# A fused attention and feed-forward kernel: the middle of its written-out order replaced

## The chip, the cores and the metric

The kernel runs on one core of one Trainium2 chip. The metric is device time in microseconds (us) of one execution. A core has five engines that run side by side, each with its own queue of instructions, executed in order: TensorE (PE, with its weight loads as PEld), VectorE (DVE), ScalarE (ACT), GpSimd (POOL) and SyncE (SP). SP and GpSimd issue nearly all DMA transfers here. An engine that waits for a semaphore holds up everything behind it in its own queue.

## The reference

Eight batches of eight heads, 576 positions, head size 64. Each batch goes through Nystrom attention with 32 landmarks, and all results through a two-layer feed-forward net with a SiLU between.

```python
q_lm = q.reshape(B, H, 32, S // 32, D).mean(axis=3)
k_lm = k.reshape(B, H, 32, S // 32, D).mean(axis=3)
A  = softmax(scale * q    @ k_lm.T)
Bm = softmax(scale * q_lm @ k_lm.T)
C  = softmax(scale * q_lm @ k.T)
Z = Bm.T / (norm1(Bm) * norminf(Bm) + 1e-6)
for _ in range(6):
    Z = 2 * Z - Z @ Bm @ Z
x = (A @ Z @ C @ v)              # -> 4608 tokens x 512
h = x @ w_in                     # 512 x 2048
out = (h * sigmoid(h)) @ w_out   # 2048 x 512
```

## The kernel before

All work is cut into named steps, and the order of all steps is written out by hand in one string, `SEQUENCE`. `Plan.run` reads it word by word. A word is a step's name, a dot and its batch; a slash gives the engine where a step may run on two; `<x` adds a wait for the step x (a gate). Each engine gets its steps in the order in which they stand in the string, and `tc.manual_schedule` emits them so; true data dependences are added by the framework as semaphore waits. The string fixes which of the eight PSUM banks a product gets.

The steps of batch b that matter here, with the lines of their code:

- `ldTGH.b` (L400): GpSimd loads half (H) of head group G of k (T=1) or q (T=0), 144 KB, cast to bf16 on the way, into the buffer `qk` that batches b and b+2 share. `ldvA.b` (L417) loads a third of v, 192 KB.
- `xtTG.b` (L553): SP issues a DMA transpose of one loaded group into `qT`. Batches 0 to 2 transpose on TensorE instead.
- `lraT`, `lrbT`, `lrcT`, `lrdT` (L592): four adds on DVE that sum `qT` to the landmarks of k or q; each `lraT` needs both groups of T. `ltrT` and `sb` on TensorE, `lmT` (a copy) and `pb` (ACT, exp) follow.
- `pbs`, `pbr`, `bmx`, `bmt`, `bbd`, `n1`, `nrm`, `stf`, `stz` (DVE): the normalised Bm and the start of the inverse. Then six rounds of `fbI` (DVE, L702), `nsI` (TensorE) and `nsdI` (DVE, L727).
- `A`, `C` (TensorE), `Ax`, `Cx` (ACT, exp), `S` (TensorE, row sums), `Ln`, `Rs` (ACT) and `etn` (DVE, L778): the two softmaxes.
- `ctG.b` (L831): SP issues a DMA transpose of the exponentials `ce` into `ct`. `cv` (TensorE) multiplies them by v; `wc` (DVE, L862) scales the result; `zbd` (DVE), `zt` (TensorE) and `ztc` (a copy) join it with the inverse; `mF` (TensorE) multiplies by w_in, and `mcFG` copies its two halves to `m`.
- `hN.b` (TensorE, two products of 512 columns) and `hx`: the first layer, `m` times `etn`. `gN`, `gx` (ACT, L932, L955): SiLU.
- `ssI`, `p1` to `p7`, `c1`, `u2`, `c5`, `c11`, `c12`, `c21`, `c22` (L1029 to L1087): the second layer, by Strassen's seven products of eight matmuls with 256 columns for each pair of token tiles. `@5320` names batch 3, pair 20. `os@` (L1000) is a group of four stores of 64 KB each, issued by SP, from one of eight buffers `ost`.

Around the change the order has a habit: the kinds of transfer take turns. `xt` and `ct` are gated on the last load before them, and the first load of a group on a transpose before it (`ld100.5<xt10.4`, `xt11.5<ldv1.5`). Gates are emitted as a dependence whose reason is given in the code as "one kind of transfer at a time":

```python
for x in o.after:
    tc.add_manual_dep(o.ins, x.ins.name, ..., reason="one kind of transfer at a time")
```

Of the kernel before, what the change touches and what calls it, by code (L numbers as in the profile page):

```python
# [65 lines left out]
ld111.4 c11@5120.0 os@5101.0 ldv1.4<xt00.3 ns00.3 m0.2 mc01.2/DVE ld000.4<xt00.3 p7@5120.0 ld001.4
nsd00.3 h4.2 c5@5120.0/DVE fb10.3 c22@5120.0 Rs0.3 Rs1.3 h7.2 wrc.3 ns10.3 ld010.4 g7.2 ld011.4
h10.2 mc00.2/ACT p4@5120.0 c21@5120.0/ACT nsd10.3 fb20.3 ns20.3 nsd20.3 ldv0.3 os@5100.0 h5.2
h14.2 g5.2 fb30.3 ns30.3 hx0.2 h8.2 g10.2 ldv2.3 gx0.2 h15.2 nsd30.3 fb40.3 g8.2 h12.2 g12.2
ldv2.4<xt00.3 g15.2 ct1.3<ldv1.4 ns40.3 nsd40.3 ct0.3<ldv1.4 xt00.4<ldv1.4 h9.2 g9.2 g14.2 h1.2  # L70
h0.2 g1.2 g0.2 fb50.3 ss30@5120.0 ns50.3 nsd50.3 zbd.3 h11.2 g11.2 h13.2 h3.2 cv0.3 h2.2 wc.3 g4.2
g13.2 g3.2 etn1.3 zt.3 ztc.3/DVE etn0.3 p3@5120.0 c12@5120.0 m3.3 mc30.3/ACT m0.3 mc01.3/DVE
mc00.3/ACT m2.3 mc21.3/ACT m1.3 mc20.3/ACT hx8.2 g2.2 h6.2 g6.2 mc31.3/DVE h12.3 gx8.2 h3.3 h10.3
mc10.3/DVE mc11.3/DVE h7.3 h2.3 g2.3 h4.3 g4.3 g10.3 h13.3 h5.3 g5.3 hx8.3 gx8.3 g13.3 h9.3 h11.3
g7.3 h14.3 h6.3 g6.3 g11.3 p1@5200.0 g3.3 h8.3 g8.3 ss00@5200.0 p5@5200.0 hx0.3 g14.3 g9.3
ss00@5220.0 xt11.4<ldv1.4 xt01.4<ldv1.4 xt10.4<ldv1.4 ld100.5<xt10.4 ld101.5 ld110.5 ld111.5
ldv0.4 ldv1.5 ld000.5 ld001.5 ld010.5 ld011.5 ss10@5200.0 lra1.4 lrb1.4 lrc1.4 ss10@5220.0
ss20@5220.0 lrd1.4 lra0.4 lrb0.4 os@5020.0 ss20@5200.0 l1done.2 ltr1.4 h1.3 h0.3 g0.3 g1.3 g12.3
h15.3 gx0.3 c1@5200.0/DVE p6@5200.0 u2@5200.0/ACT os@5021.0 ss30@5200.0 c5@5200.0/DVE p3@5200.0
ss30@5220.0 lmT1.4/DVE lrc0.4 lrd0.4 ltr0.4 lmT0.4/ACT g15.3 p1@5220.0 sb.4 pb.4 c1@5220.0/ACT  # L80
xt11.5<ldv1.5 xt10.5<ldv1.5 c12@5200.0 p7@5200.0 c22@5200.0 p2@5200.0 c11@5200.0 p4@5200.0
c21@5200.0/ACT p6@5220.0 xt01.5<ldv1.5 pbs.4 u2@5220.0/ACT pbr.4 l1done.3 bmx.4 bmt.4 bbd.4
ss00@5300.0 xt00.5<ldv1.5 C.4 lra1.5 csb.4 os@5120.0 Cx10.4 os@5121.0 Cx00.4 f0.4 p5@5220.0 Cx11.4
p7@5220.0 n1.4 lrb1.5 lrc1.5 os@5200.0 Cx01.4 nrm.4 ct0.4<ldv1.5 lrd1.5 c5@5220.0/ACT stf0.4 A.4
Ax00.4 Ax01.4 p5@5300.0 ltr1.5 fb00.4 Ax10.4 p3@5220.0 S10.4 Ln10.4 Ax11.4 wrc.4 stz.4 p1@5300.0
ns00.4 ss10@5300.0 ss20@5300.0 ss30@5300.0 c1@5300.0/ACT S00.4 S11.4 c22@5220.0 lra0.5 p4@5220.0
Ln11.4 Rs1.4 p6@5300.0 nsd00.4 lrb0.5 lrc0.5 lrd0.5 S01.4 fb10.4 lmT1.5/DVE ld000.6<xt00.5 ltr0.5
p2@5220.0 u2@5300.0/ACT p7@5300.0 ss00@5320.0 Ln01.4 c12@5220.0 lmT0.5/DVE sb.5 c21@5220.0/ACT
ns10.4 p1@5320.0 Ln00.4 ld001.6 ld010.6 Rs0.4 ld011.6 ct1.4<ldv1.5 ldv0.5<ct1.4 ldv2.5 ld100.6
ld101.6 ld110.6 ld111.6 etn1.4 pb.5 ss20@5320.0 c11@5220.0 etn0.4 pbs.5 pbr.5 p2@5320.0 nsd10.4  # L90
c1@5320.0/ACT fb20.4 bmx.5 c11@5320.0 c5@5300.0/ACT p3@5300.0 c12@5300.0 c22@5300.0 C.5 Cx01.5
cv0.4 wc.4 ldv1.6<xt00.5 bmt.5 Cx11.5 ns20.4 os@5201.0 p6@5320.0 nsd20.4 fb30.4 os@5221.0
ss10@5320.0 A.5 os@5220.0 ss30@5320.0 Cx10.5 u2@5320.0/ACT p5@5320.0 Ax11.5 csb.5 Ax01.5 bbd.5
ns30.4 Ax10.5 p7@5320.0 nsd30.4 S11.5 fb40.4 ns40.4 Ax00.5 p1@5340.0 n1.5 nrm.5 stz.5 f0.5 nsd40.4
Ln11.5 c5@5320.0/ACT fb50.4 S10.5 Ln10.5 ns50.4 ss00@5340.0 p3@5320.0 p4@5300.0 stf0.5 c22@5320.0
Rs1.5 S00.5 S01.5 Cx00.5 nsd50.4 fb00.5 Ln01.5 c12@5320.0 ns00.5 ss20@5340.0 zbd.4 p2@5300.0 zt.4
nsd00.5 fb10.5 ns10.5 c11@5300.0 p4@5320.0 wrc.5 c21@5300.0/ACT etn1.5 nsd10.5 p5@5340.0 fb20.5
Ln00.5 l1done.7 ct0.5 ztc.4/ACT c1@5340.0/ACT c21@5320.0/ACT Rs0.5 ss10@5340.0 m3.4 mc30.4/ACT
m1.4 mc31.4/DVE m2.4 mc21.4/ACT p6@5340.0 mc11.4/DVE ns20.5 mc20.4/ACT p2@5340.0 nsd20.5
mc10.4/ACT h5.4 fb30.5 ns30.5 c5@5340.0/DVE nsd30.5 h7.4 h4.4 h9.4 ct1.5 u2@5340.0/ACT g5.4 g7.4  # L100
fb40.5 ns40.5 nsd40.5 fb50.5 p7@5340.0 ss30@5340.0 ns50.5 nsd50.5 c22@5340.0 h14.4 h12.4 g4.4
zbd.5 m0.4 g9.4 g12.4 mc00.4/ACT mc01.4/DVE cv0.5 wc.5 h11.4 h1.4 g11.4 g14.4 c11@5340.0
xt00.6<ldv1.6 zt.5 p3@5340.0 ztc.5/DVE etn0.5 g1.4 ldv0.7<xt00.6 c12@5340.0 ldv1.7<xt00.6 m0.5
ldv2.7<xt00.6 ld100.7<xt00.6 ld101.7 mc01.5/ACT m3.5 mc00.5/ACT ld110.7 ld111.7 m1.5 ldv2.6<xt00.5
mc10.5/ACT xt10.6<ldv1.6 l1done.6 xt11.6<ldv1.6 ldv0.6<xt00.5 ld000.7<xt00.6 mc11.5/DVE h0.4 h10.4
mc30.5/DVE h13.4 ld001.7 g10.4 g13.4 h4.5 ld010.7 g0.4 h15.4 h7.5 g15.4 ld011.7 xt01.6<ldv1.6 h6.4
g6.4 mc31.5/DVE h14.5 h2.4 h8.4 g4.5 os@5320.0 g2.4 lra1.6 lrb1.6 os@5301.0 lrc1.6 lrd1.6 lra0.6
lrb0.6 g7.5 ltr1.6 h15.5 lrc0.6 m2.5 lmT1.6/DVE lrd0.6 g8.4 h3.4 h12.5 hx0.4 g3.4 mc21.5/DVE hx0.5
mc20.5/DVE h8.5 ss00@5400.0 gx0.4 ss20@5400.0 ss10@5400.0 gx0.5 h2.5 g2.5 h11.5 hx8.5 ltr0.6 g11.5
g8.5 p4@5340.0 h1.5 h5.5 g15.5 g12.5 gx8.5 lmT0.6/DVE sb.6 g14.5 g5.5 os@5300.0 hx8.4  # L110
c21@5340.0/DVE ss00@5420.0 p1@5400.0 gx8.4 p5@5400.0 ss30@5400.0 c1@5400.0/ACT p6@5400.0 l1done.5
ss20@5420.0 ss30@5420.0 ss10@5420.0 c5@5400.0/DVE pb.6 u2@5400.0/DVE A.6 Ax00.6 Ax11.6 p3@5400.0
h3.5 Ax01.6 pbs.6 pbr.6 bmx.6 csb.6 p1@5420.0 Ax10.6 h13.5 n1.6 g13.5 os@5321.0 c1@5420.0/DVE
h10.5 nrm.6 g10.5 p7@5400.0 h9.5 c12@5400.0 stz.6 bmt.6 bbd.6 S01.6 g3.5 S10.6 c22@5400.0 g1.5
f0.6 stf0.6 fb00.6 h6.5 h0.5 ns00.6 p6@5420.0 g9.5 xt00.7<ldv1.7 nsd00.6 fb10.6 ns10.6 g0.5 g6.5
u2@5420.0/ACT S00.6 nsd10.6 p5@5420.0 fb20.6 Ln10.6 ns20.6 p7@5420.0 c5@5420.0/ACT ss00@5500.0
xt10.7<ldv1.7 ss20@5500.0 S11.6 nsd20.6 Ln01.6 ss10@5500.0 Ln11.6 xt01.7<ldv1.7 xt11.7<ldv1.7
fb30.6 os@5341.0 p4@5400.0 Ln00.6 Rs0.6 c22@5420.0 c21@5400.0/ACT lra1.7 lrb1.7 lrc1.7 lrd1.7
lra0.7 lrb0.7 lrc0.7 os@5340.0 lrd0.7 C.6 Cx00.6 Cx11.6 Cx01.6 Cx10.6 wrc.6 p1@5500.0 Rs1.6
c1@5500.0/ACT p3@5420.0 c12@5420.0 p2@5500.0 p2@5420.0 ltr1.7 ns30.6 lmT1.7/ACT c11@5500.0  # L120
ct1.6<ldv1.7 ltr0.7 p4@5420.0 lmT0.7/ACT sb.7 p6@5500.0 nsd30.6 fb40.6 c11@5420.0 pb.7
c21@5420.0/ACT etn0.6 ss00@5520.0 ns40.6 etn1.6 A.7 pbs.7 u2@5500.0/ACT Ax01.7 Ax10.7 p5@5500.0
p7@5500.0 Ax00.7 S10.7 S01.7 c5@5500.0/ACT S00.7 ct0.6<ldv1.7 nsd40.6 Ln10.7 p2@5400.0 ss30@5500.0
fb50.6 ns50.6 pbr.7 bmx.7 Ln00.7 bmt.7 Ln01.7 csb.7 nsd50.6 n1.7 zbd.6 os@5401.0 Ax11.7 bbd.7
c11@5400.0 cv0.6 wc.6 c22@5500.0 C.7 nrm.7 p3@5500.0 Cx01.7 zt.6 f0.7 Cx11.7 ztc.6/ACT Cx10.7
ss20@5520.0 stf0.7 p4@5500.0 Cx00.7 c12@5500.0 S11.7 Ln11.7 ss10@5520.0 m1.6 os@5400.0 m0.6 m2.6
mc20.6/ACT mc21.6/ACT mc11.6/ACT mc10.6/DVE mc00.6/DVE p1@5520.0 wrc.7 stz.7 fb00.7 p2@5520.0
ns00.7 mc01.6/ACT nsd00.7 p5@5520.0 fb10.7 c1@5520.0/ACT ns10.7 Rs0.7 ct0.7 c11@5520.0 p6@5520.0
c5@5520.0/ACT nsd10.7 fb20.7 ns20.7 c21@5500.0/DVE h0.6 h5.6 h7.6 nsd20.7 h10.6 Rs1.7 g5.6 h3.6
ct1.7 etn1.7 fb30.7 ns30.7 g7.6 ss30@5520.0 os@5501.0 h4.6 nsd30.7 u2@5520.0/ACT g10.6 g0.6 hx0.6  # L130
fb40.7 ns40.7 nsd40.7 fb50.7 p7@5520.0 ns50.7 m3.6 g4.6 c22@5520.0 gx0.6 nsd50.7 cv0.7 wc.7 zbd.7
# [1060 lines left out]
```

## Time and profile before

| | us |
|---|---|
| median of 3 runs | 239.73 |
| lowest, highest | 238.82, 241.90 |
| the profiled execution | 238.85 |
| its span (first to last instruction) | 237.1 |

The profiled execution is 1.75 us longer than its span, for what lies around it. The page of the profile gives busy time by engine, the span in forty slices, the DMA queues, the chain of work that ended last and the costliest groups of instructions. Views of the trace give windows, waits, or instructions in order of time, and for DMA the time from issue to landing. The names in them are the program's tiles: `qT<-qk` is an `xt`, `ct<-ce` a `ct`, `qk<-in_k_dram` a load of k, `v<-in_v_dram` a load of v, `out_dram<-ost` a store, `red<-qT` an `lra`, `fb<-st` an `fb`, `ps<-etn,m` an `h`, `ps<-v,ct` a `cv`.

### The profile page before, as it was taken

The numbers are of one execution on the slowest core, as the hardware profiler recorded it, in microseconds if no ns is written. First come the engines' busy times: TensorE is split into PE (matmuls) and PEld (weight loads), VectorE is DVE, ScalarE is ACT, GpSimd is POOL, SyncE is SP. The second block draws the span as 40 slices with busy tenths as digits, with TensorE's granted clock in tenths as the row PEclk, the third lists the DMA queues.
The fourth block names the chain that finished last, engine by engine and source line by source line (L and its number), as shares of the span: only waits on it lengthen the run. The fifth ranks groups of instructions, "written<-read, shape, count | busy, mean of one in ns | idle before, by whom it ended". The sixth has DMA issues, their size and how long they took to land.

```text
span 237.1 us, 7501 instructions
## 1 busy us (share of the span) xinstructions
PE 230.2 (97%) x2951; PEld 167.6 (71%) x2951; DVE 182.2 (77%) x506; ACT 182.4 (77%) x435; POOL 49.3 (21%) x89
## 2 busy tenths in 40 slices
...
DMA  6999999999999998999999999995427440012355
GB/s 248 268 202 195 203 211 206 207 202 210 130 182 181 215 171 168 204 198 173 211 163 187 182 164 232 206 180 113 100 59 108 117 113 0 4 44 48 82 144 131
DMA packets 56227, 37.72 MB, mean 159 GB/s; under 512 B 36992, under 2 KB 47744, under 8 KB 56192
## 3 DMA queue, kind: packets, MB, share of 16 engines
...
q8 instruction: 23, 0.38, 0.7%
...
## 4 chain that ended last, share of the span: by engine, by line
PE 77%; ACT 8%; DMA 6%; DVE 4%; issue 2%; SPq 1%; DVEq 0%
PE ps L334 75%; DMA out_dram<-ost 4%; ACT gm L932 2%; DMA gm<-in_k_dram 2%; PE ps L526 1%; DVE etn L778 1%; ACT L1145 1%; ACT m L344 1%; ACT L932 1%; ACT pb L658 1%; DVE zt L346 1%; ACT gx L955 0%; DVE st L727 0%; ACT ce L804 0%; SPq L1000 0%
## 5 line engine op out<-in xcount | busy, mean ns | idle before, releaser
L932 ACT ACTIVATE gm<-ps 128x512 f16<-128x512 f32 x128 | 68.4, 630 | 6.7 <-PE ps L334 6.4
L334 PE MATMUL ps<-etn,m 128*128 128x64 bf16 (+2 forms) x566 | 71.5, 275 | 0.3
L334 PEld LDWEIGHTS <-gm 128*128 128x128 f16 x512 | 48.7, 98 | 10.2 <-issue 1.5
L334 PE MATMUL ps<-w_out_sb,gm 128*128 128x256 f16 (+1 forms) x392 | 53.1, 281 | 0.1
L334 PEld LDWEIGHTS <-m 128*128 128x128 bf16 x566 | 36.7, 98 | 22.2 <-issue 2.6
L334 PEld LDWEIGHTS <-ss 128*128 128x128 f16 x408 | 38.4, 98 | 7.2 <-issue 1.9
L334 PE MATMUL ps<-wt,ss 128*128 128x256 f16 x272 | 34.9, 273 | 0.0
L1064 DVE TENSOR_TENSOR ost<-ost,ps 128x256 f32<-128x256 f32 x51 | 20.6, 414 | 11.3 <-PE ps L334 8.0
L344 ACT COPY ost<-ps 128x256 f32<-128x256 f32 (+1 forms) x47 | 18.1, 391 | 11.8 <-PE ps L334 11.5
L346 DVE CAST m<-ps 128x512 bf16<-128x512 f32 x30 | 19.5, 685 | 3.3 <-PE ps L334 3.2
L417 POOL DMA_DIRECT2D v<-in_v_dram x24 | 14.4, 608 | 34.9 <-PE ps L334 16.4
L344 ACT CAST m<-ps 128x512 bf16<-128x512 f32 x34 | 18.5, 607 | 2.4 <-PE ps L334 2.4
L727 DVE SCALAR_TENSOR_TENSOR st<-st,ps 128x128 bf16<-128x128 bf16 (+2 forms) x54 | 13.6, 257 | 7.7 <-PE ps L334 7.3
L334 PE MATMUL ps<-w_out_sb,ss 128*128 128x256 f16 x136 | 17.6, 273 | 0.0
L400 POOL DMA_DIRECT2D qk<-in_k_dram x20 | 10.6, 548 | 29.8 <-DMA qT<-qk 16.7
L334 PE MATMUL ps<-wt,gm 128*128 128x256 f16 x120 | 15.5, 272 | 0.0
L702 DVE TENSOR_TENSOR fb<-st,hmask 128x256 bf16<-128x256 bf16 (+1 forms) x54 | 14.4, 273 | 1.2
L955 ACT ACTIVATE gx<-ps 128x512 f16<-128x512 f32 x16 | 9.9, 623 | 6.9 <-PE ps L334 6.9
L346 DVE COPY ost<-ps 128x256 f32<-128x256 f32 x23 | 9.6, 419 | 7.0 <-PE ps L334 6.6
L400 POOL DMA_DIRECT2D qk<-in_q_dram x20 | 10.6, 556 | 20.4 <-issue 12.0
L804 ACT ACTIVATE ce<-ps 128x288 bf16<-128x288 f32 x32 | 13.0, 434 | 2.3 <-PE ps L334 2.3
L769 ACT ACTIVATE ln<-ps 128x288 f32<-128x288 f32 x32 | 12.4, 448 | 2.8 <-PE ps L334 2.8
...
## 6 DMA issues: line engine op xcount, KB each, us to landing
...
```

Source lines behind the costliest of these rows:

```text
L334: nc.tensor.matmul(out=out_ap, lhsT=lhsT, rhs=rhs, start=start, stop=stop, skip_group_check=True)
L344: return nc.scalar.copy(out=out, in_=in_)
L346: return nc.vector.tensor_copy(out=out, in_=in_)
L400: lambda e, t=t, g=g, h=h, src=src: nc.gpsimd.dma_start(out=qk_r[b % 2][64 * h:64 * h + 64, t, g].rearrange("p j d -> p (j d)"), in_=src[b ...
L417: lambda e, a=a: nc.gpsimd.dma_start(out=v_r[b % 2][a * L:(a + 1) * L, :, :], in_=v[b].rearrange("h (l a x) d -> a l h (x d)", l=L, a=VA)[ ...
L702: nc.vector.tensor_tensor(out=fb[it % 2][:, g0:g1], in0=bc(sr[it % 3][:, g0:g1, 0:L], 4, 2), in1=bc(hmask, n, 1), op=OP.mult), [o], 14.5 + ...
L727: nc.vector.scalar_tensor_tensor(out=s2[:, g0:g1, lo:SW], in0=s[:, g0:g1, lo:SW], scalar=2.0, in1=ps[:, 0:NG * SW].rearrange("p (g x) -> p ...
L769: lambda e, g=g, c=c, ln=ln: nc.scalar.activation(out=ln[:, c], in_=bank(me["S", g, c])[:, 0:HS], func=AF.Ln),
L804: nc.scalar.activation(out=ce[:, :, 0:VP].rearrange("p (i c) (a l) -> p c a i l", c=2, a=VA)[:, c], in_=bank(me["C"], 2 * g + c)[:, 0:HS]. ...
L932: lambda e, dc=dc, cell=cell: nc.scalar.activation(out=gm[:, dc, :], in_=bank(cell["o"]), func=AF.Silu),
L955: lambda e, d0=d0, cell=cell, c=c: nc.scalar.activation(out=gx[:, d0:d0 + 8, c:c + 64].rearrange("p d (x c) -> p d x c", c=2) if b >= B - ...
L1064: nc.vector.tensor_tensor(out=out_, in0=x, in1=y, op=OP.add)
```

## The change

Only the string `SEQUENCE` changes, and in it the words from just behind `C.3 zt.2` to `ldv1.6`, before `h11.4`. By the times of the profile that is from 70 to 136 us. No step is added or left out; the words before and behind are the same.

- Loads and stores: the first ten loads go out in another order, with new gates. `ld111.6` stands behind them and in front of batch 5's loads; it overwrites what `xt11.4` reads. `ld111.5` is gated on `xt01.4`. Loads of batch 6 stand among those of batch 5, and `ldv0.4` is gated on the store `os@5120.0`.
- Transposes: `xt11.4` and `xt10.4` come first, then two store groups, then `xt01.4` and `xt00.4`; `xt00.4` is gated on `ld111.6`. In batch 5 the pairs come as `xt10 xt11`, a store group, `xt01 xt00`. `ct0.3` is gated on `ld111.4`.
- Some gates name transfers that ended long before, such as `ldk10`, a load at the very start.
- Twenty evictions from PSUM change engine: eleven from DVE to ACT, nine from ACT to DVE.
- Products stand in another order: `cv0.3` has nine `h` of batch 2 ahead of it in place of fourteen; `cv0.4` stands behind `ns50.4` in place of `C.5`; the pair products of batches 2 and 3 are spread otherwise.
- On DVE `lra1.4` and `lrb1.4` stand ahead of `etn0.3`, and `lra0.5` to `lrc0.5` ahead of `stf0.4`.

What each of the two DMA queues issues, from the first difference (cut to the changed words):

```diff
 SP
-os@5001.0 os@5000.0 os@5101.0 os@5100.0 ct1.3<ldv1.4 ct0.3<ldv1.4 xt00.4<ldv1.4 xt11.4<ldv1.4
-xt01.4<ldv1.4 xt10.4<ldv1.4 os@5020.0 os@5021.0 xt11.5<ldv1.5 xt10.5<ldv1.5 xt01.5<ldv1.5
-xt00.5<ldv1.5 os@5120.0 os@5121.0 os@5200.0 ct0.4<ldv1.5 ct1.4<ldv1.5 os@5201.0 os@5221.0
-os@5220.0 ct0.5 ct1.5
+os@5001.0 os@5000.0 ct0.3<ld111.4<ld000.4 os@5101.0 ct1.3 xt11.4<ld010.4 xt10.4<ld010.4 os@5100.0
+os@5020.0 xt01.4<ld010.4 xt00.4<ld111.6<ldv2.3 os@5021.0 xt10.5<ld101.6 xt11.5<ld111.6 os@5121.0
+xt01.5 xt00.5<ld001.5 os@5120.0 ct1.4<ld011.6 ct0.4<ld011.6 os@5220.0 os@5221.0 os@5200.0
+ct1.5<ldv2.5<ldv0.5 os@5201.0 ct0.5<ld011.5
 xt00.6<ldv1.6 xt10.6<ldv1.6
 POOL
 ld100.4<ct0.2
-ld101.4 ld110.4 ld111.4 ldv1.4<xt00.3 ld000.4<xt00.3 ld001.4 ld010.4 ld011.4 ldv0.3 ldv2.3
-ldv2.4<xt00.3 ld100.5<xt10.4 ld101.5 ld110.5 ld111.5 ldv0.4 ldv1.5 ld000.5 ld001.5 ld010.5 ld011.5
-ld000.6<xt00.5 ld001.6 ld010.6 ld011.6 ldv0.5<ct1.4 ldv2.5 ld100.6 ld101.6 ld110.6 ld111.6
-ldv1.6<xt00.5
+ld000.4<ldk10 ld001.4<xt01.3<ldk10 ld101.4<ldk11<xt00.3 ld111.4<os@5001.0 ld011.4<xt00.3
+ld110.4<os@5000.0<xt00.3 ldv0.3<os@5000.0<ldk00 ld010.4<os@5001.0 ldv2.3<ldk00<xt10.3
+ld111.6<os@5101.0 ld000.5 ld111.5<xt01.4<os@5101.0 ld110.5<os@5001.0 ld101.6<xt10.4
+ld001.5<xt10.4<ct0.3 ldv1.4<xt00.4<os@5000.0 ld101.5<ct1.3 ld100.5<os@5101.0
+ld011.5<os@5101.0<os@5021.0 ld010.5<os@5000.0 ld011.6<xt11.4<os@5101.0 ldv2.4<os@5021.0
+ldv0.4<os@5120.0 ld000.6 ldv2.5 ld110.6<xt11.5<xt00.5 ldv0.5<os@5121.0 ld100.6<os@5121.0<xt00.5
+ldv1.5<xt00.5 ld010.6<xt11.5<xt01.5 ld001.6<ct0.4 ldv1.6
 ldv0.7<xt00.6
```

And DVE's order at the two places that the prediction follows:

```diff
-wc.3 etn1.3 ztc.3 etn0.3 c12@5120.0 mc01.3 mc31.3 mc10.3 mc11.3
+wc.3 c12@5120.0 lra1.4 lrb1.4 etn0.3 mc31.3 mc30.3 lrc1.4 lrd1.4 lra0.4
...
-lra1.5 n1.4 lrb1.5 lrc1.5 nrm.4 lrd1.5 stf0.4 fb00.4
+lra1.5 lrb1.5 n1.4 nrm.4 lrc1.5 bmt.4 c22@5220.0 bbd.4 lrd1.5 ss00@5320.0 lra0.5 lrb0.5 lrc0.5
+stf0.4 fb00.4
```

180 lines of the change are left out of this document (92 added, 88 removed).

## The prediction

> **What bounds the kernel now.** The page first: span, engines, DMA. Then the windows table over most of the stretch that the change rewrites (70 to 140 us).
>
> ```profile
> span 237.1 us, 7501 instructions
> PE 230.2 (97%) x2951; PEld 167.6 (71%) x2951; DVE 182.2 (77%) x506; ACT 182.4 (77%) x435; POOL 49.3 (21%) x89
> DMA  6999999999999998999999999995427440012355
> ```
>
> ```profile
> 85.00:90.00 5.00, 4.66 (x108) 2.47 (x107) 3.48 (x7) 4.38 (x10) 0.00 (x0) 1.00 1.20 186
> 90.00:140.00 50.00, 50.00 (x632) 36.60 (x629) 42.98 (x119) 40.50 (x102) 14.30 (x27) 1.00 1.06 183
> ```
>
> TensorE is the bound: busy 97% of the span at the full granted clock. The columns of the second view are window, its length, then busy time of PE, PEld, DVE, ACT and POOL, the clock, the DMA share and GB/s. DMA is full too: its share is above 1 in both windows, so transfers queue behind each other. An order that leaves the products as they are can only win what TensorE still waits. The waits of the weight loads show that better than busy PE, because a matmul's modelled end hides a short stall (70 to 140 us):
>
> ```profile
> PEld L334 <- DVE wsb L862: 0.9, 2, 0.7
> PEld L334 <- DVE fb L702: 0.5, 2, 0.3
> PEld L334 <- DMA ct<-ce: 0.5, 1, 0.5
> PEld L334 <- ACT m L344: 0.3, 1, 0.3
> PEld L334 <- DVE pbs L667: 0.2, 1, 0.2
> PEld L334 <- DVE zt L346: 0.2, 1, 0.2
> ```
>
> Together 2.6 us, 1.1% of the span. That is the most the change can give. By the busy PE row it would be 0.34 us (5.00 less 4.66). The Trainium skill (Trainium Kernel Development and Optimization, Performance Expectations) calls matmul busy time a bad metric for the distance to the roofline; the two sums here agree with that. What TensorE waits for longest stands in the timeline:
>
> ```profile
> 82.80 1.46 PE L334 MATMUL ps<-etn,m 128*128 128x512 bf16 x6
> 85.68 0.44 PEld L334 LDWEIGHTS <-ct 96*32 96x32 bf16 x48 [0.53 <-DMA ct<-ce]
> 87.00 0.11 PEld L334 LDWEIGHTS <-wsb 128*128 128x128 bf16 x2 [0.72 <-DVE wsb L862]
> ```
>
> The value product cv.3 waits 0.53 us for the transposed ct.3; zt.3, right after it, waits 0.72 us for the eviction of cv.3 (wc.3).
>
> **What is moved, queue by queue.** No instruction is added or removed. On SP and GpSimd the order and the gates of stores, loads and transposes change:
>
> ```profile
> 64.69 13.81 SPq L1000 DMA_DIRECT2D out_dram<-ost  x16
> 79.34 3.69 SPq L831 DMA_TRANSPOSE ct<-ce  x2
> 83.14 6.54 SPq L553 DMA_TRANSPOSE qT<-qk  x4
> 89.73 3.90 SPq L1000 DMA_DIRECT2D out_dram<-ost  x8
> 100.88 6.26 SPq L553 DMA_TRANSPOSE qT<-qk  x4
> 130.68 5.97 SPq L553 DMA_TRANSPOSE qT<-qk  x4
> ```
>
> ```profile
> 67.42 2.11 POOL L400 DMA_DIRECT2D qk<-in_k_dram  x4 [7.92 <-PE ps L334]
> 92.20 2.10 POOL L400 DMA_DIRECT2D qk<-in_k_dram  x4 [16.66 <-DMA qT<-qk]
> ```
>
> Before, the kinds take turns: ct.3, four transposes of batch 4, eight stores, then a burst of ten loads from 92.20, and only after it the transposes of batch 5 at 100.88. Now SP issues os@5001.0, os@5000.0, ct0.3, os@5101.0, ct1.3, xt11.4, xt10.4, os@5100.0, os@5020.0, xt01.4, xt00.4, os@5021.0, xt10.5, xt11.5, os@5121.0, xt01.5, xt00.5, os@5120.0. GpSimd issues ten loads from 67.42 as SP frees them, then ld111.6 behind the landing of xt11.4 and ld000.5, then ld111.5 behind the landing of xt01.4; behind that gate stand ten more loads. Behind the new gate of ct0.3 on ld111.4 stand os@5101.0 and ct1.3, behind that of xt00.4 on ld111.6 os@5021.0 and batch 5. Prices, each the landing time of one transfer after its issue: a load that opens a burst; a transpose in a stretch without loads; ct.5 among loads; a store without loads; stores among loads.
>
> ```profile
> DMA to landing us min/median/max: 3.3/3.3/3.3
> DMA to landing us min/median/max: 3.4/3.5/4.4
> DMA to landing us min/median/max: 5.7/6.0/6.4
> DMA to landing us min/median/max: 1.7/1.7/3.0
> DMA to landing us min/median/max: 4.7/6.4/6.9
> SPq L553 <- DMA v<-in_v_dram: 7.1, 1, 7.1
> ```
>
> The last row is the wait of the transposes of batch 5: it ended at 100.88 with the burst's sixth load, 8.7 us after 92.20. Less 3.3 for the first, five more loads took 5.4, so 1.07 us each.
>
> **TensorE.** The products of one h by their group (70 to 140 us; busy, mean ns of one):
>
> ```profile
> L334 PE MATMUL ps<-etn,m 128*128 128x512 bf16 x83 | 20.2, 379 | 0.0
> ```
>
> Six in a row took 1.46 us, so each starts (1.46 - 0.38) / 5 = 0.216 after the last, and an h, two of them, costs 0.43. Of the fourteen h that stood ahead of cv.3 from 70 us on, nine are left; the pair products and the rest are the same. So TensorE gets there 5 x 0.43 = 2.2 us earlier than 85.68 less its wait of 0.53: at 83.0. ct1.3 must have landed by then. On SP: ct0.3 waits for ld111.4, the fifth load from 67.42, 67.42 + 3.3 + 4 x 1.07 = 75.0. A ct takes half of 2.54 to 3.69 us to issue, say 1.5, a group of four stores half of 3.90. So os@5101.0 is issued from 76.5 to 78.5, and ct1.3 at 78.5. It lands after 3.5 to 6.0 us, 82.0 to 84.5: a wait of 0 to 1.5 where 0.53 stood. I take 0.5. The 0.72 at zt.3 goes, since h3.2 and p3@5120.0 now stand between cv.3 and zt.3 (about 0.43 + 0.87 of work, against 0.42 for the eviction). What is late next is DVE.
>
> **DVE, in order.** lra1.4 and lrb1.4, which sum the transposes xt11.4 and xt10.4, now stand ahead of etn0.3 and of the evictions of m3.3; behind them waits TensorE with h13.3. SP reaches xt11.4 at 80.5 (SP is free at 80.0; the gate, ld010.4, is the ninth load, 67.42 + 3.3 + 8 x 1.07 = 79.3, and I allow 1.2 for the stores among them), xt10.4 at 82.1, landed 85.6 by 3.5. DVE comes to it at about 86.0, after p3@5120.0 and its eviction: 0.4 in hand. Then lra1.4 0.68, lrb1.4 about 0.4, etn0.3 and two evictions of m3.3:
>
> ```profile
> L346 DVE CAST m<-ps 128x512 bf16<-128x512 f32 x30 | 19.5, 685 | 3.3 <-PE ps L334 3.2
> ```
>
> With etn0.3 taken at 0.7 too (it has 576 columns) that is 86.0 + 0.7 + 0.4 + 3 x 0.7 = 89.2. TensorE has ten products of about an h ahead of h13.3 after p3@5120.0 ends at 85.5, so wants it at 89.8: another 0.6 in hand. If xt10.4 takes ct.5's 6.0 it lands 2.5 later, and 1.5 us are lost.
>
> The second place is xt00.5. SP: xt10.4 ends 83.7, two store groups to 87.6, xt01.4 to 89.2, landed 91.1; it opens the burst of eleven: 91.1 + 3.3 + 6 x 1.07 = 100.8 for the seventh, ld100.5, which xt10.5 needs (100.88 before). Four transposes and os@5121.0 between them take 6.26 + 1.95, of which the last 1.6 are its own issue, so xt00.5 is issued at 107.4 and lands at 110.9. DVE needs it at lra0.5, in the middle of the inverse's chain of batch 4:
>
> ```profile
> 107.21 1.03 PE L334 MATMUL ps<-wt,ss 128*128 128x256 f16 x8
> 108.08 1.04 PE L334 MATMUL ps<-w_out_sb,gm 128*128 128x256 f16 x8
> 112.28 0.22 PE L334 MATMUL ps<-st,fb 128*128 128x64 bf16 x2
> ```
>
> ```profile
> 111.69 0.42 DVE L1064 TENSOR_TENSOR ost<-ost,ps 128x256 f32<-128x256 f32 x1
> 112.03 0.68 DVE L592 TENSOR_TENSOR red<-qT 128x1024 f16<-128x1024 bf16 x1
> 112.83 0.74 DVE L592 TENSOR_TENSOR red<-red 128x512 f16<-128x512 f16 x2
> 113.61 0.29 DVE L592 TENSOR_TENSOR rs<-red,qT 128x256 f16<-128x256 f16 x1
> 113.81 0.28 DVE L702 TENSOR_TENSOR fb<-st,hmask 128x256 bf16<-128x256 bf16 x1
> 114.35 0.68 DVE L1029 TENSOR_TENSOR ss<-gm 128x1024 f16<-128x1024 f16 x1
> ```
>
> A pair product takes 0.87 (108.08 less 107.21). p7@5220.0 (108.08 to 109.12) has one more ahead of it, so ends near 109.9. Then DVE: c22 0.42, bbd.4 0.29 (the fb form), lrd1.5 0.29, ss00@5320.0 0.68: lra0.5 at 111.4 at the earliest, behind xt00.5's 110.9. After it 0.68 + 0.74 + 0.29, stf0.4 (about 0.2) and fb00.4 0.28: 113.6. TensorE wants ns00.4 at 112.28 + 1.9 (two pair products and a few small ones more ahead of it) = 114.2, less what was won before. So 0.5 + 0.6 us are in hand: a slip of xt00.5 by 1 us is free, beyond that it is lost one to one, as TensorE is full and in order. Before, ns00.4 stood far behind its own fb00.4, and no transpose lay in between.
>
> **Engines swapped.** Twenty evictions change engine, eleven to ACT and nine to DVE; each has its work beside TensorE's on engines that are 86 and 81% busy (42.98 and 40.50 of 50). I cost them at nothing; a wrong one would show as a TensorE wait like the 0.3 for ACT m, so between a gain of 0.3 and a loss of 0.6 (two such).
>
> **Batch 6.** Its eight q and k loads go out earlier, but ldv1.6, on which its transposes are gated, overwrites the v that cv.4 reads. Before, cv.4 stood here:
>
> ```profile
> 119.59 0.56 PE L334 MATMUL ps<-v,ct 96*32 96x64 bf16 x48
> ```
>
> Five pair products more now stand ahead of it (4.4, and A.5): about 125.0. ldv1.6 lands 3.3 after it ends, so xt00.6 starts near 129 in place of 130.68: nothing lost, and TensorE wants nothing of it sooner.
>
> **Sum** against the profiled run (238.85 us for a span of 237.1; the median of three is 239.73, 0.9 above it): -0.72 at zt.3, 0 at cv.3, up to +0.6 for DVE's in-order waits at lra1.4 or lra0.5, of which I take 0.4: -0.3, 238.5 in that run's terms, 239.4 in the median's.
>
> **Rivals.** *DMA slows when kinds mix (slower).* For it: 6.0 against 3.5 for a transpose among loads, 6.4 against 1.7 for stores, and a DMA share above 1. Place: xt01.4 (+2.5), which opens the burst; xt00.5 (+2.5); and the four loads of the burst behind its seventh, which now run beside the transposes of batch 5 (half of 4 x 1.07 if two queues share evenly: 2.1). Together 7.1, less the 1.1 in hand: +6.0, 245.7 (the 0.7 won at zt.3 is lost in this wait). It decides from a slip of xt00.5 of 5.9 us, since 2% is 4.8. With the transposes alone late, 5.0 - 1.1 = +3.9, 243.6, inside 2%. The Trainium skill (DMA: Bandwidth & Descriptors, Issuing engines are not separate DMA queues) states that transfers from all issuing engines run on the same 16 DMA engines and interleave, so mixing buys no bandwidth; the rows above agree, as each kind is slower beside the other. *All waits go.* -2.6, 237.1 in the median's terms; against it, four of the six rows of waits are for DVE and ACT chains that stay. *The order changes little.* Several gates name transfers long finished (the first loads of k), so the kinds may still land nearly in turn: 239.7.
>
> **Numbers.** The forecast, with at most 1.5 us to either side, 0.60; little change 0.08; all waits gone 0.05; transposes late, +1.5 to +4.8, 0.12; the full slowdown 0.15. The range from 237.3 to 244.5 leaves out the last. Faster by over 2% would need 234.9, more than all waits: 0.02. Slower by over 2% (above 244.5): 0.15. Two per cent is about what a measurement of this kernel tells from no change; its three runs span 238.82 to 241.9.
>
> **What would show it.** Right: cv.3 starts near 83 to 84 with a wait under 1 us, no wsb wait of 0.7 after it, red<-qT (lra0.5) near 111.4, and PEld waits in the stretch of about 2 us. Wrong: a DVE gap before red<-qT ended by DMA qT<-qk, and TensorE waiting for fb behind it; transposes landing in 6 us; xt10.5 issued after 103.

## The result and the profile after

The changed kernel takes 243.73 us, median of six runs (241.99 to 244.32); the kernel before, run beside it, 239.39 (238.82 to 241.9). The ratio is 1.0162, with a 95% interval of 1.0131 to 1.0193: slower, by less than 2%. The forecast, 0.3 us faster, had the wrong sign. Single executions are now and then some per cent longer at a lower granted clock; the medians in this document contain them, the ratios and intervals do not.

The profiled execution of the changed kernel took 242.16 us for a span of 240.4; it is one of the lower of the six. In code, every line behind the string has moved down by 4 (L334 is now L338). Of its page:

```profile
span 240.4 us, 7508 instructions
PE 231.0 (96%) x2951; PEld 167.5 (70%) x2951; DVE 180.7 (75%) x504; ACT 182.5 (76%) x437; POOL 49.3 (21%) x89
```

The work is the same; TensorE idles longer. Its waits from 70 to 140 us (weight loads, as before the change; the first row is of the kernel before, and the prediction shows its other rows):

```profile
PEld L334 <- issue: 5.3, 21, 0.4
```

```profile
PEld L338 <- issue: 8.0, 25, 1.2
PEld L338 <- DVE fb L706: 1.4, 5, 0.4
PEld L338 <- ACT m L348: 0.5, 1, 0.5
PEld L338 <- ACT gm L936: 0.4, 1, 0.4
PEld L338 <- DVE zbd L871: 0.2, 1, 0.2
PEld L338 <- DVE st L731: 0.2, 1, 0.2
```

The rows for `wsb` and `ct` are gone, as forecast. The row for `fb` grew from 0.5 to 1.4, and the one that names no releaser ("issue": the columns are us in total, times, longest) from 5.3 to 8.0, with a single stand of 1.2. Where that is, VectorE's timeline shows (start, duration, engine, line, operation, tiles; in brackets the idle time ahead of it and its end):

```profile
111.07 0.68 DVE L1033 TENSOR_TENSOR ss<-gm 128x1024 f16<-128x1024 f16 x1
114.01 0.69 DVE L596 TENSOR_TENSOR red<-qT 128x1024 f16<-128x1024 bf16 x1 [2.25 <-DMA qT<-qk]
114.73 0.75 DVE L596 TENSOR_TENSOR red<-red 128x512 f16<-128x512 f16 x2
115.40 0.22 DVE L711 TENSOR_TENSOR st<-ps,pbs 128x64 bf16<-128x64 f32 x1
115.66 0.29 DVE L706 TENSOR_TENSOR fb<-st,hmask 128x256 bf16<-128x256 bf16 x1
...
116.01 0.41 DVE L1068 TENSOR_TENSOR ost<-ost,ps 128x256 f32<-128x256 f32 x1
```

The second row is `lra0.5`. It stands 2.25 us for the transpose `xt00.5`, and `stf0.4`, `fb00.4` and the eviction `c12@5220.0` (the last three rows) stand behind it. TensorE's timeline has the other end:

```profile
115.67 0.41 PE L338 MATMUL ps<-et,hmask 128*128 128x288 bf16 x2 [1.06 <-DVE st L711]
116.47 0.22 PE L338 MATMUL ps<-st,fb 128*128 128x64 bf16 x2 [0.40 <-DVE ost L1068]
```

`S10.4` wants the PSUM bank that `stf0.4` frees, and `ns00.4` the bank that `c12@5220.0` frees. A second loss stands on ScalarE, ahead of its first SiLU of batch 4, and on TensorE behind that:

```profile
131.45 0.37 ACT L348 COPY ost<-ps 128x256 f32<-128x256 f32 x1 [0.72 <-DMA out_dram<-ost]
...
135.43 0.37 ACT L348 COPY ost<-ps 128x256 f32<-128x256 f32 x1 [0.29 <-DMA out_dram<-ost]
135.82 1.28 ACT L936 ACT_TABLE_LOAD   x1
137.12 0.60 ACT L936 ACTIVATE gm<-ps 128x512 f16<-128x512 f32 x1
```

```profile
137.76 1.07 PE L338 MATMUL ps<-etn,m 128*128 128x512 bf16 x4 [0.37 <-ACT gm L936]
```

The two copies are `c1@5340.0` and `c5@5340.0`; each overwrites an output tile that a store has not finished reading. In the kernel before, the same stretch of ScalarE has no such wait and the SiLU begins 3.5 us earlier:

```profile
131.92 0.41 ACT L344 COPY ost<-ps 128x256 f32<-128x256 f32 x1
132.36 1.28 ACT L932 ACT_TABLE_LOAD   x1
133.65 1.09 ACT L932 ACTIVATE gm<-ps 128x512 f16<-128x512 f32 x2
```

A yardstick for all that follows is the time between the starts of `C.3` and `h1.4` on TensorE (of their first weight loads): both orders have the same 149 steps of TensorE in it, and the words behind are the same. It is 67.03 us before (70.06 to 137.09) and 69.92 after (70.77 to 140.69). So 2.9 us are lost in it. By the windows view TensorE stands still for 2.20 us of the stretch (69.93 less 67.73 busy) where it was 0.34 before (67.03 less 66.69); so 1.9 of the 2.9 us are standing time, and the rest shows only in the rows of the weight loads. Another 0.7 was there at `C.3`, where the code is still the same, and 0.3 comes back at the very end, which makes the 3.3 between the two profiled runs. (In the traces of the other versions `C.3` starts between 70.07 and 71.72, a spread in which the change has no part.)

### The profile page after: what moved, and what is told of

The parts are those of the page before. It is cut to its first block, busy times and chain, and to the rows that moved or that the text cites. A ratio compares the mean times of both kernels' runs of the same rounds, so it can differ in the third digit from the quotient of the medians.

```text
span 240.4 us, 7508 instructions
## 1 busy us (share of the span) xinstructions
PE 231.0 (96%) x2951; PEld 167.5 (70%) x2951; DVE 180.7 (75%) x504; ACT 182.5 (76%) x437; POOL 49.3 (21%) x89
## 4 chain that ended last, share of the span: by engine, by line
PE 62%; ACT 11%; DMA 8%; SPq 8%; DVE 6%; issue 3%; DVEq 0%; ACTq 0%
PE ps L338 61%; SPq L1004 4%; ACT gm L936 4%; DMA gm<-in_q_dram 3%; DMA out_dram<-ost 3%; SPq L557 3%; DMA qT<-qk 2%; ACT L936 1%; ACT L1149 1%; ACT ost L348 1%; ACT pb L662 1%; DVE etn L782 1%; DVE st L731 1%; ACT m L348 1%; DVE fb L706 1%
## 5 line engine op out<-in xcount | busy, mean ns | idle before, releaser
L936 ACT ACTIVATE gm<-ps 128x512 f16<-128x512 f32 x128 | 69.1, 658 | 5.2 <-PE ps L338 4.9
L338 PE MATMUL ps<-etn,m 128*128 128x64 bf16 (+2 forms) x566 | 72.3, 275 | 0.7 <-ACT gm L936 0.4
L338 PEld LDWEIGHTS <-gm 128*128 128x128 f16 x512 | 48.4, 98 | 11.2 <-issue 2.1
L338 PE MATMUL ps<-w_out_sb,gm 128*128 128x256 f16 (+1 forms) x392 | 53.4, 281 | 0.1
L338 PEld LDWEIGHTS <-m 128*128 128x128 bf16 x566 | 36.3, 98 | 23.0 <-issue 3.8
L338 PEld LDWEIGHTS <-ss 128*128 128x128 f16 x408 | 38.5, 98 | 7.3 <-issue 2.1
L338 PE MATMUL ps<-wt,ss 128*128 128x256 f16 x272 | 34.5, 273 | 0.3 <-ACT ln L773 0.2
L348 ACT CAST m<-ps 128x512 bf16<-128x512 f32 x38 | 21.2, 625 | 1.8 <-PE ps L338 1.8
L350 DVE CAST m<-ps 128x512 bf16<-128x512 f32 x26 | 17.0, 684 | 3.0 <-PE ps L338 3.0
L338 PE MATMUL ps<-w_out_sb,ss 128*128 128x256 f16 x136 | 17.6, 273 | 0.0
L350 DVE COPY ost<-ps 128x256 f32<-128x256 f32 x24 | 10.1, 420 | 8.3 <-PE ps L338 6.1
L338 PE MATMUL ps<-wt,gm 128*128 128x256 f16 x120 | 15.5, 273 | 0.0
L596 DVE TENSOR_TENSOR red<-qT 128x1024 f16<-128x1024 bf16 x12 | 8.3, 688 | 6.9 <-DMA qT<-qk 6.7
```

The lines of the kernel that those rows point to most:

```text
L338: nc.tensor.matmul(out=out_ap, lhsT=lhsT, rhs=rhs, start=start, stop=stop, skip_group_check=True)
L348: return nc.scalar.copy(out=out, in_=in_)
L350: return nc.vector.tensor_copy(out=out, in_=in_)
L936: lambda e, dc=dc, cell=cell: nc.scalar.activation(out=gm[:, dc, :], in_=bank(cell["o"]), func=AF.Silu),
```

## The experiments

Theory 1: VectorE's wait for a late transpose, passed on to TensorE, is the loss (first seen at `lra0.5`; 1b is the same at `lra1.4`). Theory 2: ScalarE has too much to do ahead of its first SiLU; theory 3, formed later: it waits there for stores. The rival to all of them is that transfers of mixed kinds slow each other, wherever it shows.

All are compared with the kernel before, run beside them. Its median was between 238.90 and 239.57 there, so two versions are compared by their ratios, not by their medians. "Stretch" is the yardstick in the one profiled run of each.

| run | median, us | ratio, 95% interval | stretch, us |
|---|---|---|---|
| changed kernel again | 243.77 | 1.0168 [1.0122, 1.0214] | 71.31 |
| a_lra_later | 243.29 | 1.0147 [1.0095, 1.0200] | 69.57 |
| b_store_later | 243.65 | 1.0157 [1.0110, 1.0204] | 72.49 |
| c_act_lighter | 244.91 | 1.0207 [1.0149, 1.0264] | 72.08 |
| d_lra14_later | 245.73 | 1.0243 [1.0182, 1.0304] | 70.61 |
| e_both_later | 242.43 | 1.0140 [1.0102, 1.0177] | 69.59 |
| x_dma_of_after | 242.26 | 1.0131 [1.0103, 1.0159] | 69.56 |
| x_compute_of_after | 245.39 | 1.0277 [1.0236, 1.0318] | 72.91 |
| s_stores_sooner | 248.42 | 1.0404 [1.0378, 1.0430] | 76.12 |
| g_three_mended | 249.52 | 1.0438 [1.0374, 1.0502] | 76.83 |
| g_and_store_later | 249.63 | 1.0424 [1.0358, 1.0490] | 75.69 |
| f_ct0_ungated | 243.81 | 1.0192 [1.0121, 1.0262] | 70.48 |
| s2_store_after_ct | 242.74 | 1.0106 [1.0017, 1.0194] | 70.20 |
| k2_no_lra_wait | 243.02 | 1.0114 [1.0026, 1.0203] | 72.07 |
| m_loads_after_ct | 245.17 | 1.0213 [1.0130, 1.0296] | 71.93 |
| k4_all_mended | 242.98 | 1.0119 [1.0034, 1.0204] | 70.02 |
| k5_last_store | 250.17 (245.33 to 251.79) | not given | 67.29 |
| k6_second_gate | 241.99 | 1.0096 [1.0062, 1.0129] | 67.36 |

### The same kernel again, and one wait at a time

> The changed kernel once more, beside the three that follow. All theories: 1.013 to 1.019 of the kernel before. If the 1.6 us between its lowest runs (242.0) and the others (243.7 to 244.3) is a second course that the order itself can take, it shows again; if it was that chip, it does not.

Its trace has a wait that the first one hasn't, at the place that the prediction walked first. VectorE, TensorE, and the landing times of the transposes from 82 to 92 us:

```profile
89.59 0.69 DVE L596 TENSOR_TENSOR red<-qT 128x1024 f16<-128x1024 bf16 x1 [2.28 <-DMA qT<-qk]
...
91.32 1.28 DVE L350 CAST m<-ps 128x512 bf16<-128x512 f32 x2
```

```profile
92.06 1.24 PE L338 MATMUL ps<-etn,m 128*128 128x512 bf16 x5 [2.03 <-DVE m L350]
```

```profile
DMA to landing us min/median/max: 3.3/3.3/5.0
```

`xt10.4` landed at 89.5, in 5.0 us, instead of 86.4 in 3.6; `lra1.4` held the evictions of `m`, and `h6.2` waited for a bank. It began far ahead of that, in code that both kernels share: `ct0.2` landed at 69.72 instead of 67.12, and the loads of batch 4, gated on it, went out 2.6 us later. The new gate of `ct0.3` on `ld111.4` and SP's order behind it carry that on to `xt10.4`. The traces of c_act_lighter and m_loads_after_ct below took the same course: `ct0.2` landed at 70.16 and 68.58, `xt10.4` at 90.09 and 89.06, and `h6.2` stood 2.29 and 2.14. So the changed order has at least two courses. In this one the late TensorE meets a landed `xt00.5`: `S10.4` waits for nothing.

Three single edits ran beside it.

```diff
 a_lra_later: DVE
-lra0.5 lrb0.5 lrc0.5 stf0.4 fb00.4 stz.4
+stf0.4 fb00.4 lra0.5 lrb0.5 lrc0.5 stz.4
 b_store_later: SP
-os@5121.0 xt01.5 xt00.5
+xt01.5 xt00.5 os@5121.0
 c_act_lighter: ACT to DVE
-mc11.4/ACT mc31.4/ACT c5@5340.0/ACT
+mc11.4/DVE mc31.4/DVE c5@5340.0/DVE
```

> DVE's order alone: lra0.5, lrb0.5 and lrc0.5 move behind stf0.4 and fb00.4, so that a late xt00.5 holds nothing of batch 4's inverse. Theory 1 (DVE's wait at lra0.5, 2.25 us in the trace, passed to S10.4 and ns00.4): S10.4 starts at once, 1.2 to 1.8 us less than the changed kernel. Rival (the mixed DMAs slow the whole stretch, the wait at lra0.5 is only where it shows): the products behind stall instead, no change within 0.5.

The wait at `S10.4` went (0.01 us), but the interval holds that of the changed kernel. VectorE and TensorE:

```profile
113.89 0.69 DVE L594 TENSOR_TENSOR red<-qT 128x1024 f16<-128x1024 bf16 x1 [1.57 <-DMA qT<-qk]
...
115.42 0.41 DVE L1066 TENSOR_TENSOR ost<-ost,ps 128x256 f32<-128x256 f32 x1
```

```profile
115.88 0.22 PE L336 MATMUL ps<-st,fb 128*128 128x64 bf16 x2 [1.23 <-DVE ost L1066]
```

`xt00.5` is as late as ever; what stands behind `lra0.5` now is `c12@5220.0`, and `ns00.4` waits for that bank instead.

> SP's order alone: the store os@5121.0 (1.9 us of issue) moves behind xt00.5. Theory 1: xt00.5 is issued 1.9 us sooner and lands near 112.0 in place of 113.9, lra0.5 starts near 112.1 and S10.4 waits 0 to 0.3 instead of 1.24: 1.2 to 1.8 us less than the changed kernel. Rival (transposes beside loads are slow whatever the order): xt00.5's landing moves by under 0.7, and the time by under 0.7.

`xt00.5` landed at 112.52 and `S10.4` waited for nothing, as theory 1 expected; the time did not move. In this profiled run `ct0.3` took 9.2 us and `ct1.3` 7.1, the weight loads of `cv0.3` stood 2.2 for the two, and ScalarE stood 1.91 and 1.73 at the two copies. What one edit frees, another late transfer takes.

> Engines alone: mc11.4, mc31.4 and c5@5340.0 go from ACT to DVE, where the kernel before had them. Theory 2 (ACT is late at its first SiLU, 137.1, and h5.4, ns50.5 and h14.4 wait 0.3 to 0.55 each for its banks): g7.4 starts 1.0 to 1.4 sooner and the time falls by 0.6 to 1.0. Rival (PE arrives there late anyway, since the loss at 114 to 117 sets it): no change within 0.3.

Not faster, so theory 2 got no support; but this trace can't refute it. It took the course of the second trace (`h6.2` stood 2.29 us), `c5@5340.0` on VectorE waited 0.18 us for its store, and TensorE 0.85 for a cast of `m` on VectorE. That the stores make ScalarE late, and not its share of the work, is shown by k5_last_store below, where ScalarE's order is the changed kernel's and the wait is gone.

### VectorE's waits moved

```diff
 d_lra14_later and e_both_later: DVE
-lra1.4 lrb1.4 etn0.3 mc31.3 mc30.3 lrc1.4
+etn0.3 mc31.3 mc30.3 lra1.4 lrb1.4 lrc1.4
 e_both_later: DVE
-lra0.5 lrb0.5 lrc0.5 stf0.4 fb00.4 stz.4
+stf0.4 fb00.4 stz.4 lra0.5 lrb0.5 lrc0.5
```

> DVE's order alone: lra1.4 and lrb1.4 move behind mc31.3, mc11.3 and mc30.3. In the second trace of the changed kernel xt10.4 landed at 89.5 instead of 86.4, DVE stood 2.28 us at lra1.4, and h6.2 waited 2.13 for a bank that those evictions free. Theory 1b (that wait is the 1.6 us between the changed kernel's lower and its usual runs): the median falls by 1.2 to 2.0, to about 242, and runs of 244 are gone. Rival (the later DMAs of the same chain set the time, the wait only moves): under 0.5.

(`mc11.3` runs on ScalarE; the two casts in the diff are the ones that move.) Not faster: 243.08 in the profiled run, 245.3 and more in the others. In its trace no cast waits for `xt10.4`, and `S10.4` waits 1.85 us instead of 1.06, since TensorE gets there sooner and `xt00.5` doesn't. Why the other runs were longer than the changed kernel's isn't shown by that one trace; it stays open.

> DVE's order alone, in two places: lra1.4 and lrb1.4 behind the three evictions as in the other run, and lra0.5, lrb0.5, lrc0.5 behind stz.4 (one step further than the first trial, in which ns00.4 still waited 1.44 us for the bank that stz.4 frees). Theory 1 with 1b: no late transpose holds TensorE any more, 3.0 to 3.8 us less than the changed kernel's usual 243.7, so 240.0 to 240.7. Rival (products and evictions in the new order, not the DMA waits, cost about half): 241.5 to 242.5.

The median lies in the rival's range; by the ratios (1.0140 and 1.0162, in each other's intervals) it is 0.5 us less than the changed kernel, where 3.0 to 3.8 was expected. `ns00.4` still waited 0.91 us, and the trace names `c12@5220.0`; that the bank was `stz.4`'s was my misreading. The rest stood at the copies: 1.36 us for a store at `c1@5340.0`.

### The two halves of the change

One kernel has SP's and GpSimd's order of the changed kernel and the three compute engines' order of the kernel before; the other has it the other way round.

> SP's and GpSimd's order (loads, stores, transposes, with their gates) of the changed kernel, TensorE's, ScalarE's and VectorE's order of the kernel before. Theory 1 (a late transpose costs only where DVE's order puts its folding ahead of an eviction that TensorE waits for): lra1.4 stands 7 us later there, so 0 to 2 us above the kernel before (1.000 to 1.008). Rival (mixed DMAs are slower and cost the time by themselves): 3.5 to 5 above it, as the changed kernel.

3.15 us above the kernel before, somewhat under the rival's 3.5 to 5: most of the loss comes with the order of the transfers, even under the old order of products. Theory 1, in the form that a late transpose costs only in VectorE's new order, fell. The long waits on transfers from 110 to 138 us, of VectorE and of ScalarE:

```profile
DVE red L595 <- DMA qT<-qk: 1.1, 1, 1.1
```

```profile
ACT ost L347 <- DMA out_dram<-ost: 2.0, 1, 2.0
```

They are the same two: `xt00.5`, landed at 113.28 (109.12 before), and `os@5200.0`, whose four stores were landed by 131.4 (117.3 before), because SP's new order puts it behind `os@5220.0` and `os@5221.0`.

> The other half: order of SP and GpSimd of the kernel before, order of TensorE, ScalarE and VectorE of the changed one. Theory 1: xt10.4 lands last of four, at 91 to 92 as before, and lra1.4, which stands at 86.5 in DVE's order, holds its evictions till then: 4 to 6 us above the kernel before, all of it ahead of 95 us; lra0.5 does not wait. Rival (mixed DMAs): 0 to 1 above the kernel before.

6.3 us above, at the place that theory 1 named and a little more than its 4 to 6; TensorE's clock fell to half there (last section). VectorE, then TensorE:

```profile
91.33 0.69 DVE L592 TENSOR_TENSOR red<-qT 128x1024 f16<-128x1024 bf16 x1 [3.79 <-DMA qT<-qk]
```

```profile
93.80 3.39 PE L334 MATMUL ps<-etn,m 128*128 128x512 bf16 x10 [3.55 <-DVE m L346]
```

The new order of products needs `xt10.4` early; the old order of transfers brings it last. So each half loses by itself; the transfers alone lose about as much as both together (1.0131 and 1.0162, with intervals that overlap).

### The stores sooner: a transpose behind a burst of loads

```diff
 s_stores_sooner, g_three_mended, g_and_store_later: SP
-os@5120.0 ct1.4 ct0.4 os@5220.0 os@5221.0 os@5200.0 ct1.5 os@5201.0
+os@5120.0 os@5200.0 ct1.4 ct0.4 os@5201.0 os@5220.0 os@5221.0 ct1.5
 g_three_mended, g_and_store_later: DVE, besides the first edit of d
-lra0.5 lrb0.5 lrc0.5 stf0.4 fb00.4 stz.4 c12@5220.0
+stf0.4 fb00.4 stz.4 c12@5220.0 lra0.5 lrb0.5 lrc0.5
 g_and_store_later: SP, as in b
 f_ct0_ungated: SP
-ct0.3<ld111.4<ld000.4
+ct0.3
```

> SP's order alone: os@5200.0 goes directly behind os@5120.0 (it stands behind os@5220.0 and os@5221.0) and os@5201.0 behind ct0.4. In the traces of the changed kernel ScalarE stood at c1@5340.0 for 0.65 to 0.72 and at c5@5340.0 for 0.29 to 0.70 until those stores had landed, ahead of its first SiLU. Theory 3 (the late SiLU of the third place is a store's landing, which the earlier trial carried over to VectorE): no wait for a store there, 0.5 to 1.0 less than the changed kernel. Rival (ScalarE's share of the evictions makes it late): no change within 0.3.

> All three places at once: lra1.4 and lrb1.4 behind mc30.3; lra0.5, lrb0.5, lrc0.5 behind c12@5220.0 (the trial with them behind stz.4 left ns00.4 waiting 0.91 for that eviction's bank); the stores as in the other run. Theory (three in-order waits for DMAs make up the loss): 239.0 to 240.3, as the kernel before or up to 0.5% above it. Rival (the products' new order costs something by itself): 241 to 242.

> The three places mended and os@5121.0 behind xt00.5 as well. Theory: xt00.5 lands near 112, so lra0.5 does not wait even where it stands later; 0 to 0.4 below the version without it. If it is the better by more than 1, ltr0.5, which waits for lra0.5's chain, was a fourth wait.

By the ratios all three lost 5.8 us or more beside the changed kernel, which no theory had expected, and that told most. Of the first one: the landing times of `ct1.4` and `ct0.4`, then ScalarE, then TensorE.

```profile
DMA to landing us min/median/max: 6.5/8.4/10.4
```

```profile
126.92 0.41 ACT L806 ACTIVATE ce<-ps 128x288 bf16<-128x288 f32 x1 [4.62 <-DMA ct<-ce]
```

```profile
127.47 1.22 PE L336 MATMUL ps<-qT,lmT 64*32 64x288 bf16 x16 [4.35 <-ACT ce L806]
```

The four stores in front put off `ct1.4` by 0.8 us, to 115.25, and `ct0.4` to 116.52. GpSimd's burst of loads, gated on the store `os@5120.0`, had begun at 114.75. In the changed kernel `ct1.4` goes out at 114.41 and the burst begins at 115.70; there the two landed in 3.7 and 7.0 us (quoted below). Shifts of about a microsecond on both sides made `ct0.4` land 4.2 us later, and `Cx.5` on ScalarE, which overwrites what it reads, held TensorE. The windows show one thing more (the seventh value is the granted clock):

```profile
124.00:128.00 4.00, 0.53 (x8) 0.21 (x8) 0.66 (x2) 1.08 (x6) 0.53 (x1) 0.74 1.01 228
128.00:132.00 4.00, 4.00 (x32) 2.57 (x25) 0.95 (x4) 1.95 (x8) 0.00 (x0) 0.50 0.56 110
132.00:136.00 4.00, 4.00 (x84) 3.42 (x83) 2.76 (x11) 1.78 (x4) 0.60 (x1) 0.90 0.08 16
```

TensorE's clock fell to half while it stood, and stayed there for some 7 us: 0.26 of 4.00 and 0.50 of 4.00 and 0.10 of 4.00, doubled, are 6.9.

> One gate alone: ct0.3 no longer waits for ld111.4 and ld000.4 to land, so SP issues it 2 to 4 us sooner, between the loads of batch 4, and xt11.4, xt10.4 and what follows move up with it. Theory 1 (the chain from GpSimd's loads to SP's transposes is what makes xt10.4 late in the usual runs): xt10.4 lands by 86.5 in the trace, h6.2 waits under 0.3, 1.2 to 2 less than the changed kernel. Rival (mixed DMAs slow): ct0.3 takes over 7 us instead of 6, xt10.4 lands no sooner than 86.4, no gain or a loss.

Issued at 72.91 instead of 76.17, `ct0.3` took 6.9 us and `ct1.3` 8.1; `xt10.4` landed at 86.50, no sooner than 86.41. No gain: the rival, though `ct0.3` stays just under the 7 us that it named. The gate on the loads costs what it saves.

### The transfers kept apart again

```diff
 s2_store_after_ct and k4: SP
-ct0.4 os@5220.0 os@5221.0 os@5200.0
+ct0.4 os@5200.0 os@5220.0 os@5221.0
 k2_no_lra_wait and k4: DVE as in g; SP as in b
 m_loads_after_ct and k4: GpSimd
-ldv0.4<os@5120.0
+ldv0.4<ct0.4
 k5_last_store: k4, and SP
-os@5221.0 ct1.5<ldv2.5<ldv0.5 os@5201.0
+os@5221.0 os@5201.0 ct1.5<ldv2.5<ldv0.5
 k6_second_gate: k5, and GpSimd
-ldv0.7<xt00.6
+ldv0.7<xt01.6
```

> SP's order alone: os@5200.0 goes ahead of os@5220.0, but stays behind ct0.4, so that no transpose is issued later. If the store's landing at c1@5340.0 costs time by itself: no DMA wait of ScalarE there, 0.3 to 0.8 less than the changed kernel. If not (TensorE finds other work until then): no change within 0.3.

The wait at `c1@5340.0` went; at `c5@5340.0`, which needs `os@5201.0` (landed 135.75), ScalarE stood until 135.85, and `h5.4` 1.09 us behind that. The stretch is 0.3 longer than the changed kernel's first; the ratio's interval covers both.

> The two places of VectorE mended, with os@5121.0 behind xt00.5, and the stores as in the changed kernel. In the trace of the run with the stores moved too, TensorE was 1.9 us ahead of the changed kernel at ltr0.5, before ct0.4 stopped it. Theory: 241.0 to 242.0, about 2 under the changed kernel. Rival (what is won before 118 us is lost again at ct0.4, which lands at a fixed time): under 1.

By the medians 0.7 us below the changed kernel, by the ratios 1.1, in an interval that holds both 0 and 2. So the time doesn't decide; the trace speaks for the rival. `S10.4` and `ns00.4` wait for nothing, then the weight loads of `A.5` stand 1.4 us behind `ct0.4` (5.9 us to land), and the copies wait 1.58 and 0.67 for stores.

> One gate alone: GpSimd's burst from ldv0.4 on waits for ct0.4 to land, so that no load runs beside ct1.4 and ct0.4, as it was in the kernel before. If mixing slows the transposes: ct0.4 lands in 3 to 4 us instead of 6 to 7, near 119, the burst starts 3 us later, and stores and loads behind it shift. By the theory that only in-order waits cost, TensorE gains what it stands at ct0.4 in the usual runs, 0 to 1.5. If the later loads hold something: slower.

`ct1.4` and `ct0.4` land in 3.3 and 2.8 us, but the burst, and with it the gate of `ct1.5` and the store behind that gate, come later: no gain. (This trace also has the stand at `h6.2`, so it can't say how much that costs.) How much a burst does to these two transposes, in the changed kernel and in k4, where they are issued at 114.4 to 116.3 us:

```profile
DMA to landing us min/median/max: 3.7/5.3/7.0
```

```profile
DMA to landing us min/median/max: 2.8/2.8/2.8
```

> All of it: VectorE's two places, os@5121.0 behind xt00.5, os@5200.0 ahead of os@5220.0, GpSimd's burst behind ct0.4. Theory (DMA waits are the whole loss): 238.8 to 240.0, level with the kernel before. Rival (the order of products and evictions has a cost of its own): what is left above 240 is that cost, 241 to 242.

One wait was left, ScalarE's at `c5@5340.0` and TensorE's at `h5.4` behind it:

```profile
135.71 0.37 ACT L347 COPY ost<-ps 128x256 f32<-128x256 f32 x1 [2.50 <-DMA out_dram<-ost]
```

```profile
138.04 0.59 PE L337 MATMUL ps<-etn,m 128*128 128x512 bf16 x2 [2.40 <-ACT gm L935]
```

> As k4, with the store os@5201.0 directly behind os@5221.0, ahead of ct1.5 and its gate. DMA waits are the whole loss: c5@5340.0 starts near 133.3 without a wait, h5.4 waits under 0.4, 240.0 to 240.8, within 0.6% of the kernel before. Rival (the new order of products and evictions costs something by itself): the wait moves to another product, 242 to 243 as k4.

With `os@5201.0` ahead of the gated `ct1.5`, that wait is gone and the stretch is 67.29, level with before. But GpSimd's next burst, which waited for `cv0.5` in the changed kernel (140.61), now waited only for its gate on `xt00.6`. It began at 138.63, and `xt01.6` was issued at 138.90, just behind it. The copy `c5@5340.0`, the landing times of batch 6's transposes, and TensorE:

```profile
132.54 0.42 ACT L347 COPY ost<-ps 128x256 f32<-128x256 f32 x1
```

```profile
DMA to landing us min/median/max: 3.3/4.4/11.1
```

```profile
152.02 1.17 PE L337 MATMUL ps<-etn,m 128*128 128x512 bf16 x5 [5.90 <-DVE lmT L349]
```

The first half of the expectation held; one transpose, with TensorE's clock at half from 149.2 to 156 us, then made the profiled run 5 us longer than that of k4 (247.74 and 242.78).

> As k5, with GpSimd's loads from ldv0.7 on held until xt01.6 has landed, as the other burst is held until ct0.4 has. If a transpose behind a burst of loads is the cause: xt01.6 lands in 3 to 4.5 us, h12.5 waits under 0.5, and the time is 239.2 to 240.6, level with the kernel before within 0.5%. If the products' new order costs something by itself, or the held loads are missed later: 241.5 or more.

The transposes of batch 6 land in 4.8 at most, and the stretch is 67.36. The loads that were held are missed at batch 7: VectorE waits for `qT` again, and TensorE behind it.

```profile
167.37 0.69 DVE L595 TENSOR_TENSOR red<-qT 128x1024 f16<-128x1024 bf16 x1 [1.94 <-DMA qT<-qk]
```

```profile
171.08 0.28 PE L337 MATMUL ps<-rs,fold 128*128 128x256 f16 x1 [1.50 <-DVE pbs L858]
```

So the first half of the expectation held in the stretch, and the last one, that the held loads are missed later, holds in the sum. At 1.0096 it has the lowest ratio of the new order's versions, and is still slower than the kernel before. No version here is faster than that.

## Why the prediction was wrong

**TensorE as the bound, 2.6 us to win, the waits for ct.3 and wsb.** Right for the waits: both rows are gone. `cv.3` started at 84.09 in a trace that was already 0.7 late, and waited under 1 us. That 2.6 us are the most that can be won isn't shown: the sum leaves out the row that names no releaser, 5.3 us, and it is that row which grew most.

**"Another 0.6 in hand" at lra1.4.** Right in one trace (`xt10.4` at 86.41, walked to 85.6) and wrong in the other (89.49), as in those of runs c and m. The price that stood beside it, 1.5 us for a landing 2.5 later, was 2.03 for one 3.1 later. The walk took one execution's landing times as fixed.

**"So 0.5 + 0.6 us are in hand" at lra0.5: the step that failed.** `xt00.5` landed at 113.89, not 110.9. Of the 3.0 us, 1.6 were there when `xt10.5` was issued (102.36 for 100.8; the issue of the store group `os@5100.0` had held `xt01.4`, 89.79 for 87.6, and so the burst), 0.6 more when `xt00.5` was (109.59 for 107.4), and 0.8 came on its own way (4.3 us for 3.5). The wait showed where the prediction said it would, "a DVE gap before red<-qT", and TensorE lost 1.46 of VectorE's 2.25 us by it; but not only through `fb`: two PSUM banks, of `S10.4` and `ns00.4`, hung on evictions behind `lra0.5`, and the prediction had not looked for banks. That is why moving `stf0.4` and `fb00.4` alone (run a) gave nothing.

**"Engines swapped: I cost them at nothing."** The engines' load did cost next to nothing (in k5, with the swapped engines, TensorE stands still for 0.14 us of the stretch, 67.29 less 67.15 busy), but two copies, one of them swapped to ScalarE, wait for stores. The prediction followed the transposes in SP's new order and not the stores: `os@5200.0` moved from 112 to 125 us. It was a term left out, worth 0.6 us of TensorE's stands in the first trace (0.21 at 132 us and 0.37 at 137.76) and 0.8 in the second.

**The rivals.** Transposes alone late, 243.6, is where it ended; it had a chance of 0.12. Of its two places `xt00.5` is right, while `xt01.4` landed in 3.3 us, as without loads. Its reason (kinds that mix slow each other) is shown by runs s, k4 and k5, but on the way of `xt00.5` itself it made only 0.8 of the 3.0 us. That its 3.9 us agree with the 4.3 measured is partly luck: in the first trace the stores have their part of the loss, and in the second `xt10.4` makes most of it (2.03 us) and `xt00.5` none. Of the rule quoted from the Trainium skill (DMA: Bandwidth & Descriptors, Issuing engines are not separate DMA queues), the part that bears on this, transfers of all issuers sharing the same engines, agrees: the two `ct` transposes took 2.8 us alone and 6.5 and 10.4 behind GpSimd's burst.

**Shown and not shown.** Shown: with the waits on `xt10.4`, `xt00.5`, `ct0.4`, `os@5200.0` and `os@5201.0` taken away together, the stretch is within 0.3 us of the kernel before (k5 and k6, one trace each), so the order of products costs no more than about that by itself. The whole time is not won back: in k5 and k6 a transpose or a load behind the stretch is late instead. Taken away one to three at a time, they give back 1.3 us at most by the ratios, and never clear of the intervals, as the next one is already late. Only argued: why the lowest and the usual runs of the changed kernel lie 1.7 us apart. The wait at `h6.2` is of that size, and the three traces that have it with the changed transfers are of 244.04, 245.59 and 244.38 us, while the changed kernel's first trace and run a's (242.16 and 241.94) have none; but d, which takes that wait away, was not faster. Open: the long runs of d.
